# Five small reorderings in a spectral-layer-plus-FFN kernel: high parts first, scale steps on GpSimd, two preparation tables and one load moved

## The chip, the cores and the metric

The kernel runs on one core of one Trainium2 chip. The metric is the device time of one execution in microseconds (us), the median of several runs. The core's engines are named as in the profile: PE (TensorE, the matmuls), PEld (its weight loads), DVE (VectorE), ACT (ScalarE), POOL (GpSimd) and SP (SyncE, which here issues the DMA transfers). Each engine takes its instructions strictly in order; an instruction that waits holds up everything behind it on its engine.

## The reference

An input x of 8192 tokens by 448 features passes a spectral layer and a gated feed-forward layer (FFN), each with a layernorm whose scale, shift and gate come from a small condition vector c.

```python
mod = (_silu(c) @ w_mod).reshape(c.shape[0], 6, 1, -1)
sa, ca, ga, sb, cb, gb = (mod[:, n] for n in range(6))
h = _layernorm(x) * (1 + ca) + sa
x = x + ga * _A_ref(h, A_w1, A_b1, A_w2, A_b2)
h = _layernorm(x) * (1 + cb) + sb
x = x + gb * _B_ref(h, B_w_gate, B_w_up, B_w_down)

# _A_ref: rfft2 over the tokens (1 x 8192), then in 4 blocks of 112 features a complex
# two-layer MLP with biases: relu after the first layer, soft threshold (lam = 0.01)
# after the second; irfft2
# _B_ref: (gelu(x @ w_gate) * (x @ w_up)) @ w_down      448 -> 1792 -> 448
```

## The kernel before, in words

**Precision.** Matmuls run on 16-bit operands. A value that needs more is split into a high part (a cast, often on ACT) and a low part (the value minus the high part, on DVE or POOL), and both are multiplied. In the names, `hh` and `hl` are the high and low parts of the hidden layer h of the spectral MLP, `yh` and `yl` of its output y, `th` and `tl` of the transform's input t, `vh`, `gh` and `gl` of the inverse transform's input.

**The spectral stage** (about 78 to 341 us) works on 32 units (h, bt), h a half of the feature blocks and bt a group of frequencies. It is software pipelined: one step issues the transform of unit i (`stage_s2`), the first MLP layer of unit i−1 (`stage_m1`, L476 on), the second of unit i−2 (`stage_m2`), and the last transform product of unit i−3 (`stage_i1`, whose result `us` ACT copies at L589). In `stage_m1` the inner function `out` takes one bank of PSUM: ACT writes the high part with a Relu (L485), then DVE the low part (L486). The two units with bt = 0 have one frequency more (the constant term's partner) in a small bank `pmx`, and for the constant term itself ACT (L524) and DVE (L525, L526) add the biases in the same bank as the main part.

Between the steps the kernel drips in small one-off work, an entry of a list `tiny` at a time: norms of the FFN's weights, and from them scales that are powers of two. `VL` and `GL` are proxies that append an operation to that list for DVE or POOL; all these operations carry line L614. `pow2(s, bnd, p)` (L740) makes from a bound a power of two by integer arithmetic on the bits: a mask of the exponent, then a multiply-and-add. `inv_pow2` inverts such a scale with one multiply-and-add. `all_sum` (L828) adds over partitions with a small matmul that rides on another bank, whose result DVE copies out (L835). The scales are `sk` (hidden bound), `sw` (gate and up weights), `sa_act` and `isa` (activations, seven columns), `dsw`, `hs` and `ds_d` (undoing them), `dsc` (down weights).

**The FFN stage** works on 32 chunks i of two groups of tokens. Chunks 0 to 7 are in the standard form: 14 steps k of `gate_up` (L1240), two PSUM banks per step for gate and up. ACT forms gel (L1276), DVE multiplies it with the up half into x (L1281), which frees the bank; then ACT and DVE quantize x into `ac` (L1300, L1301). `down` of the chunk before (L1313 to L1315) runs after k = 2, as seven Strassen products with hooks m0, m1, m2 between them. From chunk 8 (index U0, about 745 us) on, a Strassen–Winograd form runs (`period`, L1496), with seven combined weights kept in HBM and loaded part by part (`load_part`, L1399) into a few buffers `wk`.

What else has to be done in chunks 0 to 7 stands in tables keyed by chunk and k. `start` and `steady` (into `prep`) say when each of the seven combined weights is made: `load_forms`, `form_sums` (POOL and DVE sums of raw weights `wr`), `forms_hi` (ACT) and `forms_lo` (DVE, L1728 to L1738) into `ws`, and `store_forms` to HBM (L1744). `first` says when in chunk 0 the down weights are made: `load_d8` (DMA into `dr`), `down_hi` (ACT, L1055), `down_lo` (DVE, L1059). `load_v` and `load_g` (L1028, L1020, L1022) fetch for a later chunk the inverse transform's input v, its factors g and the residual xx.

**What sets the order.** Nothing is reordered after the program is written: each engine runs its instructions in the order of the code, and SP issues the DMAs in that order too. Waits come from the framework, which tracks each buffer; for a PSUM bank that means the bank as a whole, so a reader on ACT that comes behind one on DVE in the code waits for it.

## Time and profile before

| | us |
|---|---|
| median of 3 runs (lowest, highest) | 1850.62 (1848.66, 1852.45) |
| the profiled execution | 1853.3 |
| its span (first to last instruction) | 1851.4 |
| spectral stage, from to | 78 to 341 |
| Winograd stage begins | 745 |

The profile's page gives the busy time of each engine. Its other views, which the prediction quotes, are read so. A row of the **timeline** has the start, the duration, the engine, the line, the operation, what it writes and reads, and in brackets the idle time of the engine just before it with what ended that time ("<-DVE x L1281": the engine waited for DVE's write of x on line 1281); "x8" means eight like instructions in a row, from the first one's start to the last one's end. The view of **waits** sums these idle times: in total, how often, the longest. A row of the **windows** has the busy time and the count of each engine in a stretch of time, then the granted clock of PE as a share of full speed, the busy share of the DMA engines and GB/s. Durations of pipelined instructions can overlap the next one's start a little. The page's summary by 40 slices, each 46 us, shows a steady PE from about 100 us on:

```profile
PE   7999999899999999999999999999999999999998
DVE  7788999887766667677777777777777777777755
POOL 3466878256777778777777777777777777777644
```

### The profile page before, as it was taken

What the parts mean: (1) busy time and instruction counts of PE and PEld (TensorE: products, weight loads), DVE (VectorE), ACT (ScalarE), POOL (GpSimd) and SP (SyncE); (2) the same over time, 40 slices, a digit from 0 to 9 for tenths busy, and PEclk for the clock granted to TensorE, in tenths of its full rate; (3) what the DMA queues carried; (4) which work ended last, traced back from release to release, by engine and by line L of the source; (5) the groups of instructions that cost most, each with busy time, mean ns of one, the idle gap of its engine ahead of it and who ended that gap; (6) DMA issues with size and microseconds to landing.
All of it is one profiled execution on the core that took longest, in us unless ns stands there. A gap on an engine that the chain in (4) does not pass through costs nothing.

```text
span 1851.4 us, 55998 instructions
## 1 busy us (share of the span) xinstructions
PE 1807.8 (98%) x23040; PEld 1710.9 (92%) x23040; DVE 1404.3 (76%) x2944; ACT 991.2 (54%) x1924; POOL 1316.2 (71%) x1732
## 2 busy tenths in 40 slices
PE   7999999899999999999999999999999999999998
PEld 3698989778898999999999999999999999999998
DVE  7788999887766667677777777777777777777755
ACT  5776778643434444455555555555555555555543
POOL 3466878256777778777777777777777777777644
PEclk9999999999999999999999999999999999999999
DMA  9988868654444445966666666666666666666661
GB/s 352 325 275 262 251 191 227 197 143 105 105 105 105 105 95 118 293 180 182 179 174 173 173 173 173 173 173 173 180 182 179 174 180 180 182 179 179 158 167 57
DMA packets 386232, 332.02 MB, mean 179 GB/s; under 512 B 116404, under 2 KB 364344, under 8 KB 385976
## 3 DMA queue, kind: packets, MB, share of 16 engines
q1 hardware_dynamic: 385976, 328.45, 64.4%
q8 instruction: 180, 2.95, 0.7%
q14 instruction: 76, 0.62, 0.1%
HBM read 243.32 MB, written 60.10 MB: 164 GB/s over the span
## 4 chain that ended last, share of the span: by engine, by line
PE 85%; DVE 6%; DMA 2%; POOL 2%; ACT 2%; SPq 1%; issue 1%; ACTq 0%; DVEq 0%; POOLq 0%
PE set L1496 37%; PE pgu L1240 11%; PE pdn L1313 6%; PE pdn L1315 6%; PE pdn L1314 6%; PE ps L213 2%; PE set L1313 2%; PE set L1314 2%; PE set L1315 2%; DVE y L556 1%; DVE hl L486 1%; DVE st L174 1%; PE set L1620 1%; PE pm L539 1%; PE pm L511 1%
## 5 line engine op out<-in xcount | busy, mean ns | idle before, releaser
L1496 PE MATMUL set<-nt,wk 128*128 128x128 f16 x12768 | 721.2, 219 | 3.2 <-ACT sb L1524 2.5
L1496 PEld LDWEIGHTS <-wk 128*128 128x128 f16 x12768 | 717.6, 98 | 4.8 <-issue 3.6
L1315 PE MATMUL pdn<-wd,ac 128*128 128x224 f16 x1218 | 315.5, 259 | 0.6 <-DVE ac L1301 0.6
L1313 PE MATMUL pdn<-wd,ac 128*128 128x224 f16 x1218 | 315.7, 259 | 0.0
L1314 PE MATMUL pdn<-wd,ac 128*128 128x224 f16 x1218 | 315.5, 259 | 0.0
L1240 PE MATMUL pgu<-nt,wk 128*128 128x256 f16 (+1 forms) x2464 | 269.0, 274 | 5.1 <-DVE x L1281 5.1
L1240 PEld LDWEIGHTS <-wk 128*128 128x128 f16 (+1 forms) x2464 | 226.0, 98 | 46.8 <-issue 20.9
L1545 ACT ACTIVATE gl<-c,dg 128x384 f32<-128x384 f32 x168 | 103.1, 614 | 241.4 <-DVE c L1539 238.4
L1571 DVE SCALAR_TENSOR_TENSOR ac<-x,sa_act,ac 128x896 f16<-128x896 f32 x168 | 205.0, 1220 | 35.8 <-ACT ac L1561 35.7
L1289 POOL TENSOR_TENSOR x<-x 128x128 f32<-128x128 f32 x223 | 129.5, 581 | 108.3 <-DVE x L1281 59.4
L1561 ACT ACTIVATE ac<-x,sa_act 128x896 f16<-128x896 f32 x168 | 174.8, 1040 | 54.4 <-POOL x L1292 48.2
L1290 POOL TENSOR_TENSOR x<-x 128x128 f32<-128x128 f32 x223 | 185.3, 831 | 17.5
L1359 POOL TENSOR_TENSOR cq<-cq 128x224 f32<-128x224 f32 x32 | 21.1, 658 | 246.9 <-DVE cq L1358 246.9
L1291 POOL TENSOR_TENSOR x<-x 128x128 f32<-128x128 f32 x223 | 173.1, 776 | 0.0
L1313 PEld LDWEIGHTS <-ac 128*128 128x128 f16 x1568 | 153.4, 98 | 4.9 <-issue 4.8
L1549 DVE TENSOR_TENSOR x<-c,gl 128x384 f32<-128x384 f32 x168 | 142.3, 847 | 18.4 <-ACT gl L1545 17.5
L1315 PEld LDWEIGHTS <-ac 128*128 128x128 f16 x1568 | 153.4, 98 | 0.8 <-DVE ac L1301 0.8
L1314 PEld LDWEIGHTS <-ac 128*128 128x128 f16 x1568 | 153.5, 98 | 0.1
L1292 POOL TENSOR_TENSOR x<-x 128x128 f32<-128x128 f32 x223 | 139.5, 626 | 0.0
L1533 DVE TENSOR_TENSOR c<-set,sb 128x512 f32<-128x512 f32 x168 | 115.0, 685 | 26.8 <-PE set L1496 25.3
L117 POOL TENSOR_TENSOR yl<-y,yh 128x448 fp32r<-128x448 f32 x63 | 88.2, 1417 | 54.6 <-ACT yh L115 54.3
L1276 ACT ACTIVATE gel<-pgu,dg 128x256 f32<-128x256 f32 x112 | 49.5, 471 | 140.5 <-PE pgu L1240 132.9
(346 smaller groups left out, 3786.4 us busy)
## 6 DMA issues: line engine op xcount, KB each, us to landing
wk<-wk SPq DMA_DIRECT2D x76, 1024.0 KB, 9.2
wk<-wk SPq DMA_DIRECT2D x76, 768.0 KB, 5.0
tr<-td SPq DMA_DIRECT2D x32, 448.0 KB, 4.8
vd<-us SPq DMA_DIRECT2D x64, 224.0 KB, 3.1
xx<-in_A_x SPq DMA_DIRECT2D x32, 448.0 KB, 4.2
v<-vd SPq DMA_DIRECT2D x63, 224.0 KB, 5.7
out<-x SPq DMA_DIRECT2D x31, 448.0 KB, 6.8
xt<-in_A_x SPq DMA_DIRECT2D x15, 896.0 KB, 14.9
```

What stands on the lines that cost most here:

```text
L1240: T.matmul(pgu[i, t, q][:, pr * H : (pr + 1) * H], ws[rows, n, w, tw], nts[i][rows, tn, :], start=start, stop=stop, skip_group_check=True,)
L1289: e.tensor_tensor(s1, a21, a22, ALU.add)
L1290: e.tensor_tensor(s2, s1, a11, ALU.subtract)
L1291: e.tensor_tensor(s3, a11, a21, ALU.subtract)
L1292: e.tensor_tensor(s4, a12, s2, ALU.subtract)
L1313: T.matmul(ps, ac[:, 0, ka], w[:, 0, kb], start=n == 0, stop=False)
L1314: T.matmul(ps, ac[:, 0, ka], w[:, 1, kb], start=False, stop=False)
L1315: T.matmul(ps, ac[:, 1, ka], w[:, 0, kb], start=False, stop=n == NP - 1)
L1496: T.matmul(ps2[:, pr, reg * 128 : reg * 128 + 128], slot[:, pr, hl, wt, :], nt[:, xt, :], start=start and j == 0, stop=j == len(terms) - 1 ...
L1549: V.tensor_tensor(xs[u][:, 1::3, :], cts.pop(u)[:, 1], gls.pop(u), ALU.mult)
L1561: S.activation(ac[:, 0], xs[u][:, 0:7], AF.Copy, scale=sa_act[:, t : t + 1])
L1571: V.scalar_tensor_tensor(ac[:, 1], xs.pop(u)[:, 0:7], sa_act[:, t : t + 1], ac[:, 0], op0=ALU.mult, op1=ALU.subtract)
```

## The change

It has five parts, none of which alters what is computed.

1. In `stage_m1`, `out` writes the high part and returns the low part as a function. In the units with bt = 0 both high parts of `pmx` are issued ahead of the two low parts, and ACT's bias rows (L524) ahead of the low part of their bank. The order on each engine stays the same; only who waits for whom between ACT and DVE changes.
2. `pow2` is one multiply-and-add on POOL, `inv_pow2` as well. The mask of the exponent is done on DVE: on the bound in `row_scales`, in place of the copy in `all_sum`, and on `sa_act`. Eight small operations are added on POOL.
3. The table `start`: the forms of the first combined weight are made earlier in chunk 1, most of them within the down products (m0 to m2).
4. The table `first`: the low parts 3 to 6 of the down weights, the loads 5 and 6 and the high parts 4 to 6 come later in chunk 0.
5. `load_v` and `load_g` for chunk i+3 are issued ahead of the entries of `prep` of the same k, and for i = 7 at k = 7 instead of k = 9.

```diff
                 S.activation(hhi[:BS, :, q], pv, AF.Relu)
-                V.scalar_tensor_tensor(hlo[:, :, q], pv, 0.0, hhi[:BS, :, q], op0=ALU.max, op1=ALU.subtract)
+                return lambda: V.scalar_tensor_tensor(
+                    hlo[:, :, q], pv, 0.0, hhi[:BS, :, q], op0=ALU.max, op1=ALU.subtract
+                )
...
-                for kk in range(2):
-                    out(kk, es[kk], q)
+                for low in [out(kk, es[kk], q) for kk in range(2)]:
+                    low()
...
-                out(kk, ps[:BS, : 2 * w], q)
-                if bt == 0:
+                low = out(kk, ps[:BS, : 2 * w], q)
+                if bt != 0:
+                    low()
+                else:
                     h0 = bp.tile([BS, 2], F32, tag="h0", name="h0", bufs=2)
                     for ro in range(2):
                         j = ro * NBLK + k
                         S.activation(hhi[:BS, ro, 0:1], o[ro][:, 0:1], AF.Relu, bias=hb[:, j : j + 1])
+                    low()
...
         def pow2(s, bnd, p=15):
 
             bi, si = bnd.bitcast(I32), s.bitcast(I32)
-            VL.tensor_single_scalar(si, bi, 0x7F800000, ALU.bitwise_and)
-            VL.tensor_scalar(si, si, -1.0, float((253 + p) << 23), op0=ALU.mult, op1=ALU.add)
+            GL.tensor_scalar(si, bi, -1.0, float((253 + p) << 23), op0=ALU.mult, op1=ALU.add)
 
         def inv_pow2(d, s):
-            VL.tensor_scalar(d.bitcast(I32), s.bitcast(I32), -1.0, float(254 << 23), op0=ALU.mult, op1=ALU.add)
+            GL.tensor_scalar(d.bitcast(I32), s.bitcast(I32), -1.0, float(254 << 23), op0=ALU.mult, op1=ALU.add)
...
+            bi = bnd.bitcast(I32)
+            VL.tensor_single_scalar(bi, bi, 0x7F800000, ALU.bitwise_and)
             pow2(sk, bnd, 13)
...
-                return lambda: V.tensor_copy(dst, ps[:, D : D + n])
+                return lambda: V.tensor_single_scalar(
+                    dst.bitcast(I32), ps[:, D : D + n].bitcast(I32), 0x7F800000, ALU.bitwise_and
+                )
...
+            si = sa_act.bitcast(I32)
+            VL.tensor_single_scalar(si, si, 0x7F800000, ALU.bitwise_and)
             pow2(sa_act, sa_act, 13)
...
-            ("m2", form_sums, 1),
-            ("m2", forms_hi, 1, 3),
-            (3, forms_lo, 1, 3),
...
+            ("m1", form_sums, 1),
+            ("m1", forms_hi, 1, 3, 4),
+            ("m2", forms_lo, 1, 3, 4),
...
-            4: [(pack_hi, 1), (pack_lo, 1), (down_lo, 3), (load_d8, 5)],
-            5: [(down_hi, 4)],
-            6: [(down_lo, 4), (load_d8, 6)],
-            7: [(down_hi, 5)],
-            8: [(down_lo, 5)],
-            9: [(down_hi, 6)],
-            10: [(down_lo, 6)],
+            4: [(pack_hi, 1), (pack_lo, 1)],
+            5: [(down_lo, 3), (load_d8, 5), (down_hi, 4)],
+            7: [(down_lo, 4), (load_d8, 6), (down_hi, 5)],
+            9: [(down_lo, 5)],
+            10: [(down_hi, 6)],
+            11: [(down_lo, 6)],
...
+                if k == (7 if i == NSTD - 1 else 9) and i > 0:
+                    load_v(i + 3)
+                    load_g(i + 3)
                 for fn, *args in prep.pop((i, k), []):
                     fn(*args)
...
-                if k == 9 and i > 0:
-                    load_v(i + 3)
-                    load_g(i + 3)
```

Three places show how the instructions move (line numbers of the changed kernel are some ten higher). First DVE in the spectral stage, from the sum of the weight norms (`mxa`) on to the low parts `hl` that follow the last scale, before:

```order
L835 COPY mxa<-pi_3568 128x2
L464 SCALAR_TENSOR_TENSOR zl<-ps_3588,zh_809 112x2x256
L614 TENSOR_SCALAR sw<-mxa 128x2
L464 SCALAR_TENSOR_TENSOR zl<-ps_3597,zh_810 112x2x256
L614 TENSOR_SCALAR sw<-sw 128x2
...
L464 SCALAR_TENSOR_TENSOR zl<-ps_3746,zh_812 112x2x256
L614 TENSOR_SCALAR sa_act<-sa_act 128x7 x2
L556 SCALAR_TENSOR_TENSOR y<-pm_3775,lam,t 64x224 x4
L614 TENSOR_SCALAR isa<-sa_act 128x7
L556 SCALAR_TENSOR_TENSOR y<-pm_3797,lam,t 64x224 x4
L614 TENSOR_TENSOR dsc<-dn 128x7
L486 SCALAR_TENSOR_TENSOR hl<-pm_3822,hh_813 112x2x256
```

And POOL at the same place, with the change:

```order
L117 TENSOR_TENSOR yl<-y,yh 128x448 x2
L619 TENSOR_SCALAR sw<-mxa 128x2
L619 COPY sww<-sw 64x1
L115 CAST th<-tr 128x896
L117 TENSOR_TENSOR tl<-tr,th 128x896
L619 COPY sww<-sw 64x1
L619 TENSOR_SCALAR dsw<-sw 128x2
L619 TENSOR_SCALAR hs<-sk 128x1
L619 TENSOR_SCALAR dsw<-dsw,hs 128x2
L619 COPY dg<-dsw 128x1
...
L619 TENSOR_SCALAR sa_act<-sa_act 128x7
L115 CAST th<-tr 128x896
```

The two steps of sw, those of dsw and hs, isa and one of the two of sa_act left DVE; on POOL sw, dsw, hs and sa_act now stand among the operations for th, tl and yl.

Second, DVE in chunk 1, from the first result of a down product (`cq`, seven rows for seven products) through the forms of the first combined weight (`ws`), before:

```order
L1341 TENSOR_TENSOR cq_3433<-pdn,cq_3432 128x224
L1728 SCALAR_TENSOR_TENSOR ws<-wr,sww,ws 128x3x128
L1349 TENSOR_TENSOR cq_3432<-pdn,cq_3432 128x224
...
L1368 TENSOR_TENSOR cq_3433<-pdn,cq_3432 128x224
L1281 TENSOR_TENSOR x_6750<-pgu,gel 128x2x128 x2
...
L1728 SCALAR_TENSOR_TENSOR ws<-wr,sww,ws 128x128
L1731 COPY ws<-ws 128x2x128
L1728 SCALAR_TENSOR_TENSOR ws<-wr,sww,ws 128x3x128
L1281 TENSOR_TENSOR x_6798<-pgu,gel 128x2x128
L1728 SCALAR_TENSOR_TENSOR ws<-wr,sww,ws 128x3x128
L1733 COPY ws<-ws 128x384
L1734 COPY ws<-ws 128x128
L1281 TENSOR_TENSOR x_6798<-pgu,gel 128x2x128
```

And with the change:

```order
L1351 TENSOR_TENSOR cq_3433<-pdn,cq_3432 128x224
L1738 SCALAR_TENSOR_TENSOR ws<-wr,sww,ws 128x3x128 x2
...
L1738 SCALAR_TENSOR_TENSOR ws<-wr,sww,ws 128x128
L1741 COPY ws<-ws 128x2x128
L1738 SCALAR_TENSOR_TENSOR ws<-wr,sww,ws 128x3x128 x2
L1743 COPY ws<-ws 128x384
L1744 COPY ws<-ws 128x128
L1367 TENSOR_TENSOR cq_3433<-pdn,cq_3432 128x224
...
L1291 TENSOR_TENSOR x_6805<-pgu,gel 128x2x128
L1738 SCALAR_TENSOR_TENSOR ws<-wr,sww,ws 128x3x128
L1746 COPY ws<-ws 128x128
L1738 SCALAR_TENSOR_TENSOR ws<-wr,sww,ws 128x256
```

The forms that stood around the first x of the second pair of banks now stand ahead of `cq` of the down product; the next forms took their place between the x of that pair.

Third, SP at the last standard chunk (the stores `wk_73<-ws` of the last combined weight, the loads of Winograd weights, and v, g, xx), before:

```order
L1480 DMA_TRANSPOSE nt<-pk 128x5x128 x4
L1744 DMA wk_73<-ws 64x4x384 x4
L1399 DMA wk_3420<-wk_62 128x8x512
L1399 DMA wk_3420<-wk_63 128x8x384
L1028 DMA v<-vd 128x2x224 x2
L1020 DMA g<-cgm 128x256
L1022 DMA xx<-in_A_x 128x896
L1399 DMA wk_3421<-wk_64 128x8x512
```

And with the change:

```order
L1490 DMA_TRANSPOSE nt<-pk 128x5x128 x4
L1038 DMA v<-vd 128x2x224 x2
L1030 DMA g<-cgm 128x256
L1032 DMA xx<-in_A_x 128x896
L1754 DMA wk_73<-ws 64x4x384 x4
L1409 DMA wk_3420<-wk_62 128x8x512
L1409 DMA wk_3420<-wk_63 128x8x384
L1409 DMA wk_3421<-wk_64 128x8x512
```

The v, g and xx transfers went ahead of the four stores and two loads; what stands behind them is the same.

More of the change, by code (lines that the diff above doesn't have):

```diff
@@ L1748, in spectral_geglu @@
             ("m0", form_sums, 0),
-            ("m0", forms_hi, 0),
-            ("m1", forms_lo, 0),
-            ("m1", forms_hi, 2),
-            ("m2", forms_lo, 2),
-            ("m2", form_sums, 1),
-            ("m2", forms_hi, 1, 3),
-            (3, forms_lo, 1, 3),
-            (3, forms_hi, 4),
-            (4, forms_lo, 4),
-            (4, form_sums, 2),
-            (4, forms_hi, 5),
-            (5, forms_lo, 5),
-            (5, forms_hi, 6),
-            (5, store_forms, 0),
-            (6, forms_lo, 6),
-            (6, forms_hi, 7),
-            (7, forms_lo, 7),
-            (7, forms_hi, 8),
-            (8, forms_lo, 8),
-            (9, store_forms, 1),
+            ("m0", forms_hi, 0, 2),
+            ("m1", forms_lo, 0, 2),
+            ("m1", form_sums, 1),
+            ("m1", forms_hi, 1, 3, 4),
+            ("m2", forms_lo, 1, 3, 4),
+            ("m2", form_sums, 2),
+            ("m2", forms_hi, 5),
+            (3, forms_hi, 6),
+            (4, forms_lo, 5, 6),
+            (4, store_forms, 0),
+            (4, forms_hi, 7),
+            (5, forms_lo, 7),
+            (6, forms_hi, 8),
+            (7, forms_lo, 8),
+            (8, store_forms, 1),
         ]
```

## The prediction

> **What bounds the kernel now.** I read the page's busy shares first, then the view of waits of the tensor engine (PE), then its timeline and the windows around each wait, and last the rows of the engines that each wait names.
>
> ```profile
> PE 1807.8 (98%) x23040; PEld 1710.9 (92%) x23040; DVE 1404.3 (76%) x2944; ACT 991.2 (54%) x1924; POOL 1316.2 (71%) x1732
> ...
> 821.12 29.80 PE set L1496 x532
> ...
> PE pgu L1240 <- DVE x L1281: 5.1, 7, 1.2
> PE pm L539 <- DVE hl L486: 4.2, 7, 1.7
> PE pw L819 <- ACT us L589: 4.2, 2, 2.2
> PE set L1496 <- ACT sb L1524: 2.5, 1, 2.5
> ...
> 250.00:275.00 25.00, 25.00 (x266) 24.31 (x265) 24.48 (x48) 21.36 (x40) 19.92 (x15) 1.00 0.77 212
> ```
>
> The first row is the page's; the second is a piece of the chain of work that ended last; the next four are PE's waits (total, times, longest); the last is a window of 25 us, in the order PE, weight load, DVE, ACT, POOL. PE is busy 1807.8 of 1851.4 us, so all its idle time is 43.6 us. The Strassen stage runs 532 matmuls in 29.80 us, 56 ns each, with nothing between them, and in the middle of the spectral stage PE is busy 25.00 of 25 us. So a microsecond of PE idle that goes early is carried to the end, and no more than 43.6 can go. The four rows of waits are 16.0 us together, and the change aims at them; the other 27.6 us lie at places that it does not touch.
>
> A second cost sits behind some of these waits: the granted clock (the last but two column).
>
> ```profile
> 158.70:162.10 3.40, 3.40 (x26) 2.81 (x26) 3.26 (x9) 0.63 (x1) 3.24 (x4) 0.50 0.91 230
> 244.00:247.40 3.40, 3.17 (x18) 2.61 (x18) 3.35 (x8) 1.97 (x5) 3.33 (x3) 0.50 0.58 142
> 752.60:756.00 3.40, 3.40 (x35) 3.40 (x34) 2.31 (x2) 3.40 (x10) 3.40 (x5) 0.50 1.10 334
> 170.00:173.40 3.40, 3.37 (x45) 3.08 (x45) 2.39 (x6) 2.04 (x4) 3.32 (x4) 1.00 0.54 135
> ```
>
> After the waits that end at 157.18, 243.73 and 752.47 PE runs one window of 3.4 us at 0.50; after the wait of 1.99 us that ends at 170.03 it does not. Half speed over 3.4 us is 1.7 us of work lost where PE is the bound. I take it that a drop goes with the wait ahead of it.
>
> **Part 1: constant-term units.** Two units have the extra column (bt = 0); their `stage_m1` now issues a high part (ACT) before the low part (DVE) that reads the same bank.
>
> ```profile
> ACT hh L524 <- DVE hl L486: 3.0, 4, 0.8
> ACT hh L485 <- DVE hl L486: 2.8, 2, 1.7
> ...
> 148.33 3.72 DVE L556 SCALAR_TENSOR_TENSOR y<-pm,lam,t 64x224 f32<-64x224 f32 x8
> 156.59 0.97 ACT L589 COPY us<-pi 128x448 f32<-128x448 f32 x2
> 157.18 0.34 PE L819 MATMUL pw<-onesb,sq 128*128 128x1 bf16 x8 [2.19 <-ACT us L589]
> 170.03 0.34 PE L819 MATMUL pw<-onesb,sq 128*128 128x1 bf16 x8 [1.99 <-ACT us L589]
> ```
>
> The first two rows are ACT's waits between 148 and 172 us. Per unit ACT waits for DVE once at L485 (1.7 us in one, 2.8 − 1.7 = 1.1 in the other) and twice at L524 (3.0 / 4 = 0.75 each): 3.2 us in the first unit, 2.6 in the second. Behind them on ACT stand the cast of yh and the copy us, and on us waits PE. Without them PE could go on at 157.18 − 3.2 = 153.98; it is ready at 157.18 − 2.19 = 154.99. Next late is DVE's y, which ends at 148.33 + 3.72 = 152.05; yh and us behind it, at about 1 us each (0.97), end near 154, so again in time. In the second unit us allows 170.03 − 2.6 = 167.43, against 168.04. Both waits go, with 0.6 to 1.0 us to spare: 2.19 + 1.99 = **−4.2**. No instruction is added. Bounds: half of it (−2.1) if a second dependence holds ACT, and −5.9 if the half-speed window at 158.70 is gained as well; I take none of that 1.7, since PE waits again at 170.03, so what it loses at half speed before is time that it would have waited.
>
> **Part 2: steps of the scales on POOL.** Eight integer steps on tiles of up to seven columns leave DVE; the masks stay on it, and one of them rides on a copy that is there anyway.
>
> ```profile
> 227.46 1.45 DVE L614 TENSOR_SCALAR sw<-sw 128x2 int32<-128x2 int32 x1
> 236.63 1.28 DVE L614 TENSOR_SCALAR sa_act<-sa_act 128x7 int32<-128x7 int32 x2
> 239.68 1.19 DVE L614 TENSOR_SCALAR isa<-sa_act 128x7 int32<-128x7 int32 x1
> 242.78 0.17 DVE L614 TENSOR_TENSOR dsc<-dn 128x7 f32<-128x7 f32 x1
> 242.98 0.69 DVE L486 SCALAR_TENSOR_TENSOR hl<-pm,hh 112x512 f16<-112x512 f32 x1
> ...
> 227.00 1.89 POOL L117 TENSOR_TENSOR tl<-tr,th 128x896 f16<-128x896 f32 x1
> 233.90 1.78 POOL L614 TENSOR_SCALAR dsw<-dsw,hs 128x2 f32<-128x2 f32 x1 [4.50 <-DVE hs L614]
> 240.97 0.33 POOL L614 TENSOR_SCALAR sa_act<-sa_act,dsw 128x7 f32<-128x7 f32 x1
> ...
> 240.91 0.65 PE L457 MATMUL ps<-s,tl 128*112 128x128 f16 x8 [0.27 <-POOL tl L117]
> 243.73 0.27 PE L539 MATMUL pm<-w2h,hl 112*128 112x224 f16 x1 [1.40 <-DVE hl L486]
> ```
>
> A step of 0.17 us on DVE takes 1.19 to 1.45 us while POOL runs a large operation: sw, begun at 227.46, ends at 228.91, with POOL's tl (227.00 + 1.89 = 228.89). From 235 to 243 DVE has no idle time, so each step stands ahead of hl at 242.98. Isa (1.19) and half of the pair sa_act (0.64) go: hl begins at 241.15 at the latest, 1.83 us earlier, and PE asks for it 1.40 us earlier. That wait goes. POOL gets sw, dsw, hs and sa_act ahead of the tl that PE waited 0.27 us for; POOL's own idle time of 4.50 us there (it waited for DVE's hs, which it now makes itself) holds them, at 0.33 us as in the quiet row. I take −1.3 of the waits (1.40 + 0.27, less 0.4 for steps stretched on POOL) and −1.7 for the half-speed window at 244.00: **−3.0**. Bounds: −3.4 with both waits whole, and 0 if the waits only move to POOL; beyond that the slower rival, below.
>
> [...]
>
> **Parts 3 and 4: chunks 0 and 1 of the FFN.** A gate-up bank is freed by DVE's x (L1281), which queues behind low down weights (chunk 0) or forms (chunk 1).
>
> ```profile
> 391.61 4.96 PE L1240 MATMUL pgu<-nt,wk 64*128 64x256 f16 x45 [0.29 <-DVE x L1281]
> 402.74 1.03 PE L1240 MATMUL pgu<-nt,wk 64*128 64x256 f16 x9 [1.14 <-DVE x L1281]
> 398.61 1.04 ACT L1055 ACTIVATE wd<-dr,dsc 128x896 f16<-128x896 f32 x1 [1.37 <-DMA dr<-sd]
> ...
> 438.53 0.48 PE L1240 MATMUL pgu<-nt,wk 64*128 64x256 f16 x5 [1.17 <-DVE x L1281]
> 460.44 2.77 PE L1240 MATMUL pgu<-nt,wk 64*128 64x256 f16 x25 [0.92 <-DVE x L1281]
> 433.74 2.45 DVE L1728 SCALAR_TENSOR_TENSOR ws<-wr,sww,ws 128x384 f16<-128x384 f32 x1
> 436.44 1.43 DVE L1728 SCALAR_TENSOR_TENSOR ws<-wr,sww,ws 128x384 f16<-128x384 f32 x1
> 419.48 0.39 DVE L1349 TENSOR_TENSOR cq<-pdn,cq 128x224 f32<-128x224 f32 x1 [2.17 <-PE pdn L1315]
> ```
>
> Chunk 0: the small wait at 391.61 goes (−0.29). The one at 402.74 does not: `load_d8(6)` now stands behind the later low part 4 on SP and lands about where ACT already waited 1.37 us for it (398.61), and ACT's gel and DVE's x queue behind that cast. Moved by one or two positions it costs between 0 and a further 2 us. I take **−0.4**, between −1.4 (both gone) and +1.0. Chunk 1: forms of 2.45 and 1.43 us between two x are the wait of 1.17. They move into the down products, where DVE sat 2.17 us idle before one row alone. The wait at 460.44 lies behind the chunk's last forms, which now come a k or two sooner. Of 1.17 + 0.92 I take **−1.6** (0 to −2.1): the forms of k = 4 now stand between the x of one pair, so something remains.
>
> **Part 5: inverse input earlier.** At i = 7, v, g and xx now stand ahead of four stores of forms and two loads of Winograd weights on SP.
>
> ```profile
> 740.91 4.27 SPq L1028 DMA_DIRECT2D v<-vd  x2
> 751.00 0.94 ACT L1120 CAST vh<-v 128x896 fp32r<-128x896 f32 x1 [2.81 <-DMA v<-vd]
> 752.47 7.82 PE set L1496 x108
> 735.92 2.86 SPq L1744 DMA_DIRECT2D wk<-ws  x4
> 738.00:750.00 12.00, 11.99 (x148) 10.69 (x146) 11.38 (x30) 3.42 (x6) 8.36 (x13) 1.00 1.03 294
> ```
>
> ACT waits 2.81 us for v with sb, PE's releaser, queued behind; PE waits 2.49 and runs its next 108 matmuls in 7.82 us, where 108 × 56 ns is 6.05: 1.77 us more. Issued at about 735.9, v lands five us earlier, and the stall is gone: 2.49 + 1.77 = 4.26. But the DMA engines are full (share 1.03) and the same bytes stand in the queue: the store and the weights of the second Winograd unit move back by v's 4.27 us of issuing and a little for g and xx. PE sits idle for none of them now (11.99 of 12 us busy up to 750), but how much earlier they land than they are wanted no row tells. Behind v in the queue nothing changes, so the third unit's weights land as late as before while PE comes to them 4 us sooner. A new wait may thus cost anything from nothing to all of the 4.26; I take half, **−2.1**, as neither end has the nearer row.
>
> **Sum.** −4.2 − 3.0 − 0.4 − 1.6 − 2.1 = −11.3. The profiled execution took 1853.3 us (span 1851.4), 2.7 over the median of 1850.6, and would take 1842.0; from the median it is 1839.3, which I predict. A measurement of this kernel tells about 0.2%, 3.7 us, from no change.
>
> **The rivals.** *Half speed stays* (0.12): the window at 244 or 752 comes of a shorter wait too, or of something else there. For it: 170.03 shows that a wait of 1.99 us needn't bring one, so wait and drop are not one to one. Price: 1.7 + 1.77, less the half that part 5 discounts, about 2.6: 1841.9 to 1842.8. [...]
>
> *The moved transfers take the waits' place* (0.12): chunk 0 loses 1.0 for the late down weights, part 5 and chunk 1 bring nothing. For it: full DMA engines and SP's fixed order. Sum −4.2 − 3.0 + 1.0 = −6.2: 1844.4.
>
> *Given back in the drain* (0.10): what parts 1 and 2 gain is lost again when the spectral stage ends, because its last transfers and not PE set that end. For it: of the 27.6 us of idle time elsewhere some lies there. Against it: PE, busy 25.00 of 25 us, is the bound ahead of it. Left are 0.4 + 1.6 + 2.1 = 4.1: 1846.5, at the bound of 0.2%.
>
> *The waits have twins* (0.07): the change does not do what it says, since a second condition ends within 0.3 us of each removed wait; 1850 ± 2.
>
> *Slower* (0.08): POOL's eight steps each meet a DVE operation and take 1.78 us, as dsw does at 233.90. That is 14.2 us, less POOL's idle 4.50: th, tl and yl come 9.7 us late and PE, busy 25.00 of 25 us, has no slack to take it. With −8.3 of the other parts it is +1.4, and +4.8 with the two half-speed windows that waits of this size bring by the rows above: 1855.4. The sign turns where a step takes over (4.50 + 8.3 − 3.4) / 8 = 1.2 us. Against it: 0.33 us at 240.97.
>
> **How the numbers follow.** The forecast keeps 0.51; its own range is 1834 to 1843. Faster by over 0.2% are the forecast, the first rival, most of the second (0.10) and half of the third (0.05): 0.78. Within 0.2%: 0.02 + 0.05 + 0.07 = 0.14. Slower: 0.08. All bounds at their best give −5.9 − 3.4 − 1.4 − 2.1 − 4.3 = −17.1, or 1833.5. The range of 1833.5 to 1848.5 leaves out the slower rival and the twins, 0.15, and little else.
>
> **What would show it.** PE's wait on us (4.2 us) gone from the view of waits, and with it ACT's on hl; no wait of PE over 1 us at 243 and a clock of 1.00 in the window behind; POOL's small steps at 0.2 to 0.4 us, not 1.8; no PE wait near 438; at 752 no row of 2.5 us, but one of 1 to 2 us with a DMA of wk behind it. I am wrong if PE waits for th, tl or yl in the spectral stage, if ACT waits over 2 us for dr near 400, or if the half-speed windows stay with their waits gone.

## The result, and the profile after

| | us |
|---|---|
| before, median of 5 runs (lowest, highest) | 1850.51 (1848.22, 1852.45) |
| changed, median of 5 runs (lowest, highest) | 1839.09 (1836.23, 1842.32) |
| ratio, 95% interval | 0.9939 (0.9922 to 0.9955) |
| profiled execution of the changed kernel (span) | 1839.5 (1837.4) |

The changed kernel is faster by 0.6%, 11.4 us, and its median is 0.2 us from the predicted 1839.3. How far that is luck is told below.

PE's busy time on the page and its view of waits, after:

```profile
PE 1804.2 (98%) x23040; PEld 1708.0 (93%) x23040; DVE 1400.6 (76%) x2934; ACT 991.9 (54%) x1924; POOL 1320.0 (72%) x1740
...
PE pgu L1250 <- DVE x L1291: 3.2, 3, 1.6
PE pm L544 <- DVE hl L486: 2.3, 5, 1.5
PE pi L590 <- DVE hl L486: 1.1, 2, 0.9
PE set L1506 <- DMA wk<-wk: 1.8, 2, 1.0
...
PE pw L825 <- ACT us L594: 0.7, 1, 0.7
```

The four rows at which the change aimed fell from 16.0 to 6.2 us (5.1 to 3.2 for x, 4.2 to 2.3 for hl, 4.2 to 0.7 for us, 2.5 to none for sb), while a new row of 1.8 us for the weights `wk` came and a wait on hl grew from 0.3 us (at L585) to 1.1 us (L590).

Both profiles hold the same 23040 matmuls in the same order. So the start of each matmul after, less the start of the same one before, is PE's lead at that place, and the growth of the lead over a stretch is what was gained there. I did this for the two first profiles, and again for a second profile of each kernel (below, `before_again` and `after_again`). Times of places are those of the kernel before.

| place | predicted | first pair | second pair |
|---|---|---|---|
| up to 144 us, one step of part 2 | 0 | −1.2 | −1.7 |
| part 1, 144 to 172 | −4.2 | −4.2 | −5.3 |
| part 2, 228 to 256 | −3.0 | −3.9 | −2.8 |
| drain, 325 to 362, not touched | 0 | −1.6 | −2.2 |
| part 4, chunk 0, 362 to 408 | −0.4 | +0.9 | +0.5 |
| part 3, chunk 1, 408 to 465 | −1.6 | −2.1 | −2.1 |
| part 5, Winograd entry, 742 to 770 | −2.1 | −1.8 | −2.1 |
| the rest | 0 | −0.1 | −0.3 |
| sum | −11.3 | −14.0 | −16.0 |

The first row is nearly all chance. Of the change only the step of `sk` lies there, at 102 us; with part 2 a wait of PE on hl behind it is 1.5 us instead of 1.7. The thirteen other profiles of this study lie between 0.0 and −3.9 us there against the first profile of before, and the second profile of the same kernel at −1.5. Without this row the pairs give −12.8 and −14.3, and the medians −11.4 here and −13.0 in the second measurement. One row has the wrong sign (chunk 0) and one was not foreseen (the drain).

### The profile page after: what moved, and what is told of

It is laid out like the page before. It is cut to its first block, busy times and chain, and to the rows that moved or that the text cites. A ratio compares the mean times of both kernels' runs of the same rounds, so it can differ in the third digit from the quotient of the medians.

```text
span 1837.4 us, 55986 instructions
## 1 busy us (share of the span) xinstructions
PE 1804.2 (98%) x23040; PEld 1708.0 (93%) x23040; DVE 1400.6 (76%) x2934; ACT 991.9 (54%) x1924; POOL 1320.0 (72%) x1740
## 4 chain that ended last, share of the span: by engine, by line
PE 87%; DVE 6%; DMA 2%; POOL 2%; ACT 2%; issue 1%; SPq 0%; ACTq 0%; DVEq 0%; POOLq 0%
PE set L1506 37%; PE pgu L1250 11%; PE pdn L1323 6%; PE pdn L1325 6%; PE pdn L1324 6%; PE ps L213 2%; PE set L1325 2%; PE set L1323 2%; PE set L1324 2%; DVE y L561 1%; PE set L1630 1%; PE pm L513 1%; DMA wk<-wk 1%; PE ps L451 1%; PE pm L515 1%
```

## The experiments

All of them are compared by PE's lead at each place, which resolves 0.1 us where a median of a few runs resolves about 1.5.

### Part 1 taken back

```diff
-                for low in [out(kk, es[kk], q) for kk in range(2)]:
-                    low()
+                for kk in range(2):
+                    out(kk, es[kk], q)
```

and likewise for the bias rows.

> The changed kernel with part 1 taken back (high and low parts of the constant-term units in the old order). Theory: part 1 is worth 4.6 us, because in the two traces PE's lead grows from 0.7 to 5.4 us between 150 and 170 us. Then PE's two waits on us (2.2 and 2.0 us) return, a half-speed window returns behind the first, the profiled span is 4 to 5.5 us longer than the changed kernel's 1837.4, and the drain near 331 us keeps its short waits. Rival: the spectral stage is paced elsewhere and gives part 1's lead back, so that the span is within 2 us of 1837.4.

Measured: 1844.74 us, ratio 0.9974 (0.9963 to 0.9986), span 1842.7. PE's rows of this kernel at the two waits, and the windows behind them:

```profile
155.79 0.34 PE L820 MATMUL pw<-onesb,sq 128*128 128x1 bf16 x8 [2.19 <-ACT us L589]
...
168.59 0.34 PE L820 MATMUL pw<-onesb,sq 128*128 128x1 bf16 x8 [2.00 <-ACT us L589]
...
156.72:160.13 3.41, 3.41 (x26) 2.55 (x24) 2.90 (x7) 1.07 (x2) 3.33 (x4) 0.50 0.75 188
170.37:173.78 3.41, 3.41 (x24) 2.83 (x21) 3.17 (x8) 0.69 (x2) 3.25 (x4) 0.50 0.93 248
```

Both waits are back to a hundredth, and this time both have a half-speed window behind them. Between 144 us and the end of the second window PE loses 6.8 us against the changed kernel and gets none of it back before 325 us: the spectral stage carries the lead. So the part is worth more than the 4.2 us of its waits, and what it is worth depends on the half-speed windows.

### Part 2 taken back

```diff
-            GL.tensor_scalar(d.bitcast(I32), ...)
+            VL.tensor_scalar(d.bitcast(I32), ...)
```

and `pow2` and the masks as before.

> The changed kernel with part 2 taken back (all steps of the scales on DVE again, masks as before). Theory: part 2 is worth 3.8 us at 230 to 250 us; hl near 237 to 238 us comes late again (PE wait about 1.4 us) and a half-speed window may follow it; the span is 3 to 4.5 us longer. Rival for the drain: the 1.9 us that PE won between 325 and 360 us, which the prediction did not have, also belong to part 2 (its POOL or DVE order reaches further than thought): then the span is 5 to 6.5 us longer.

Measured: 1841.73 us, ratio 0.9958 (0.9942 to 0.9974). One row of PE and two of DVE, in this kernel:

```profile
237.34 0.27 PE L544 MATMUL pm<-w2h,hl 112*128 112x224 f16 x1 [1.40 <-DVE hl L486]
...
230.24 1.27 DVE L619 TENSOR_SCALAR sa_act<-sa_act 128x7 int32<-128x7 int32 x2
...
233.29 1.19 DVE L619 TENSOR_SCALAR isa<-sa_act 128x7 int32<-128x7 int32 x1
```

The steps of 1.2 us and the wait of 1.40 are back. No half-speed window followed, and PE loses 2.8 us at this place. In `before_again` (below), which has the same wait of 1.39 us, none followed either, so the half-speed window is no fixed part of what part 2 is worth. The waits in the drain stay short (0.45 and 0.47 us at L538), so the drain's gain isn't part 2's alone, and the rival there falls.

### Part 3 taken back

> The changed kernel with part 4 taken back (the old table for chunk 0's down weights). Theory: part 4 costs time, since in the changed kernel ACT waits 1.9, 1.3 and 1.3 us for the moved loads into dr, PE waits 1.63 us at 391 us and runs a window at half speed behind it: without part 4 that wait and window go, waits of 0.3, 0.2 and about 1.1 us come back, and the span is 1 to 2.5 us shorter. Rival (the prediction): part 4 gains 0.4 us, so the span is about 0.4 us longer.

The kernel that ran is another than its expectation says: it has the old table `start` (part 3 taken back), the new table `first`, and leaves out the mask on `sa_act`, so that this scale is no power of two. It says nothing on part 4 and is read here for part 3. Measured: 1839.33 us, ratio 0.9950 (0.9935 to 0.9965). PE's waits in chunk 1:

```profile
426.75 0.48 PE L1248 MATMUL pgu<-nt,wk 64*128 64x256 f16 x5 [1.16 <-DVE x L1289]
...
448.57 1.68 PE L1248 MATMUL pgu<-nt,wk 64*128 64x256 f16 x15 [0.92 <-DVE x L1289]
```

The waits of 1.17 and 0.92 us of the kernel before are back as 1.16 and 0.92, where the changed kernel has one of 0.69. PE loses 2.0 us in chunk 1, the 2.1 that both pairs show. This profile also loses 2.5 us at the Winograd entry, which bears on part 5.

### Part 5 taken back

> The changed kernel with part 5 taken back (v, g and xx behind the stores and the weights again). Theory: PE's wait on sb of about 2.5 us returns near 741 us with a half-speed window in most phases, PE's waits of 0.99 and 0.85 us on the Winograd weights go, and the span is 1.5 to 2.7 us longer. Rival: the waits on the weights stem from the DMA volume and stay; then the span is 3 to 4.5 us longer.

Measured: 1840.76 us, ratio 0.9955 (0.9939 to 0.9971); the profiled execution was the fastest of the four, 1838.5. Its waits at the Winograd entry:

```profile
PE set L1506 <- ACT sb L1534: 1.1, 1, 1.1
PE set L1506 <- DMA wk<-wk: 1.1, 1, 1.1
```

The wait on sb is 1.1 us and not 2.5, with no half-speed window behind it, and a wait on the weights stays: at the entry this profile loses 0.1 us against the changed kernel. Neither theory gave that. Of three profiles with the old order, the wait on sb was 2.5, 2.6 (`before_again`) and 1.1 us; in the third, SP's transposes took 0.6 to 0.8 us less and v landed at least 0.5 us sooner after its issue. With the new order the entry is as uneven: PE's first wait on the weights is 0.9 to 1.3 us in four of the eight profiles that have part 5 as it is, and 1.7 to 2.1 us in the other four. In `undo4` it is 2.13 us with a half-speed window behind it, and the entry ends 0.7 us later than in the first profile of before. Against that profile, the entry brings between 1.8 us and −0.7 us with part 5, and between 1.7 and −0.3 us without it. By the medians of this kernel and of the changed one (1837.4 to 1839.1) part 5 is worth 1.7 to 3.4 us, but the intervals overlap, and this profile loses 1.8 us behind 770 us, at eleven waits of 0.11 to 0.12 us each in the Winograd stage that no other shows and whose cause is open. What part 5 is worth is therefore not settled.

### Part 4 taken back

```diff
-            4: [(pack_hi, 1), (pack_lo, 1)],
-            5: [(down_lo, 3), (load_d8, 5), (down_hi, 4)],
-            7: [(down_lo, 4), (load_d8, 6), (down_hi, 5)],
+            4: [(pack_hi, 1), (pack_lo, 1), (down_lo, 3), (load_d8, 5)],
+            5: [(down_hi, 4)],
+            6: [(down_lo, 4), (load_d8, 6)],
...
```

> The changed kernel with the table of chunk 0 alone taken back (low down weights early again; the forms of chunk 1 stay moved). In the changed kernel ACT waits 1.9, 1.3 and 1.3 us for loads into dr between 380 and 390 us and PE 1.63 us at 391. Theory A: these waits come of part 4, since its loads stand behind later low parts; then the span is 1 to 2.5 us shorter than the changed kernel's 1837.4 and PE has no wait over 1.2 us between 380 and 400. Theory B (the prediction): the table gains 0.4 us; PE then waits about 1.1 us once at a later step, and 0.2 to 0.3 us twice, and the span is within 1 us.

Measured: 1835.91 us, ratio 0.9927 (0.9912 to 0.9941). In the changed kernel, ACT's high parts of the down weights (L1065) and PE's row behind them, and the window that follows:

```profile
382.69 1.04 ACT L1065 ACTIVATE wd<-dr,dsc 128x896 f16<-128x896 f32 x1 [1.88 <-DMA dr<-sd]
...
387.08 0.85 ACT L1065 ACTIVATE wd<-dr,dsc 128x672 f16<-128x672 f32 x1 [1.33 <-DMA dr<-in_B_w_down]
389.23 1.04 ACT L1065 ACTIVATE wd<-dr,dsc 128x896 f16<-128x896 f32 x1 [1.30 <-DMA dr<-sd]
...
391.15 4.16 PE L1250 MATMUL pgu<-nt,wk 64*128 64x256 f16 x25 [1.63 <-DVE x L1291]
...
392.34:395.75 3.41, 3.41 (x16) 2.35 (x14) 3.37 (x5) 0.36 (x1) 3.01 (x3) 0.50 0.01 2
```

And PE in the same chunk with the old table:

```profile
372.68 4.85 PE L1250 MATMUL pgu<-nt,wk 128*128 128x256 f16 x43 [1.07 <-DVE x L1291]
...
388.35 2.77 PE L1250 MATMUL pgu<-nt,wk 64*128 64x256 f16 x25 [0.56 <-DVE x L1291]
```

Theory A holds: part 4 takes time. Chunk 0 takes 1.6 us less with the old table than in the changed kernel's first profile and 0.3 less than in its second. The two differ by the half-speed window alone: it follows the wait of 1.63 in the first profile and not the 1.67 in the second. Against the first profile of before, chunk 0 takes 0.7 to 1.3 us more in the five profiles that have the new table and a half-speed window there, and between 0.4 less and 0.2 more in the three without the window; with the old table (four profiles) it is never slower, and up to 0.9 us faster.

### The cause in chunk 0: high part 6 one step later

```diff
-            10: [(down_hi, 6)],
-            11: [(down_lo, 6)],
+            11: [(down_hi, 6)],
+            12: [(down_lo, 6)],
```

`best1` has this edit, with one at the Winograd entry that is read in the next part.

> As the last, but with the new table for chunk 0, in which the high part 6 comes one step later (with low part 6 behind it). Theory: in the changed kernel ACT waits 1.33 and 1.30 us in high part 6 for the late load into dr, with a gel behind it on which DVE's x and so PE's 1.63 us at 391 hang; one step later the load has landed before ACT comes to it, and the wait of PE falls below 0.5 us, with no half-speed window behind it. Rival: PE's wait hangs on DVE's low part ahead of x and stays over 1 us. The entry into the Winograd stage as in the last kernel.

The DVE row that frees PE in the changed kernel, and ACT and PE of `best1` in chunk 0:

```profile
390.67 0.42 DVE L1291 TENSOR_TENSOR x<-pgu,gel 128x256 f32<-128x256 f32 x1 [1.47 <-ACT gel L1286]
...
390.82 1.77 ACT L1065 ACTIVATE wd<-dr,dsc 128x672 f16<-128x672 f32 x2
...
385.25 7.75 PE L1250 MATMUL pgu<-nt,wk 128*128 128x256 f16 x68 [0.76 <-DVE x L1291]
```

ACT no longer waits before high part 6, and PE's 1.63 us are gone; one wait of 0.76 earlier in the chunk is left. Chunk 0 takes 2.4 and 1.1 us less than in the changed kernel's two profiles. So PE's wait in the changed kernel came through ACT: a high part that waits for its transfer, with gel queued behind it, and DVE's x behind gel.

### The Winograd entry: stores last

`best1` and `best2` (the old table for chunk 0) also change the order of SP's transfers: v, the second unit's weights, g and xx, the third unit's weights, and the four stores last. Of the edit the lines for the stores are shown; the load of g and xx moves by a like one.

```diff
-                at_k = (n, NFT + k) if type(k) is int and k < 0 else (1 + n, k)
+                late = n == NP - 1 and fn is store_forms and args == [1]
+                at_k = (n, NFT + k) if type(k) is int and k < 0 else (1 + n, 12 if late else k)
```

> Parts 1, 2 and 3 of the change and the load of v from part 5, with the old table for chunk 0, and at the entry into the Winograd stage the load of v first, then the two loads for the second Winograd unit, then g and xx (xx held SP up 1.8 us in the changed kernel), the two loads for the third unit, and the four stores last. Theory: PE's waits for these weights (1.2 and 0.8 us with the old table) come of the transfers ahead of them in SP's order, so both go or fall below 0.3 us, v still lands in time, and the time is 1 to 2 us below the kernel with the old table alone (0.9927 of the kernel before), some 4 to 5 us below the changed kernel. Rival: the DMA engines are full there, so only the order of landing changes and one of the waits stays.

Measured: `best2` 1843.26 us, ratio 0.9963 (0.9951 to 0.9974); `best1` 1841.63, 0.9954 (0.9936 to 0.9971). Both are slower than the changed kernel. ACT and PE of `best1`:

```profile
740.73 0.59 ACT L1534 COPY sb<-set 128x512 f32<-128x512 f32 x1 [9.09 <-DMA wk<-ws]
...
741.37 1.91 PE L1506 MATMUL set<-nt,wk 128*128 128x128 f16 x14 [6.60 <-ACT sb L1534]
```

Both theories are wrong. The waits on the weights are gone, but ACT's first copy into sb waits 9.09 us for the stores out of ws, and PE 6.60 us behind it. In the code ws lies in a pool that is closed before the pool of sb is opened; by this wait sb lies in memory of ws, and the stores must have read it first. So the stores can't come last: ACT and PE wait for them. No view of the kernel before shows this, since there they were done in time.

### Both corrections

`best3` has the later high part 6 and, on SP, v, the four stores, the second unit's weights, and then g and xx.

> The changed kernel with high part 6 of the down weights one step later (as in best1), and at the entry into the Winograd stage v, the four stores, the two loads for the second unit, and only then g and xx. Theory: PE's 1.63 us at 391 fall below 0.8 us and the half-speed window behind them goes; without the 1.8 us that SP waited for xx, PE's wait of about 0.9 us on the second unit's weights goes, and since the stores stay ahead of sb there is no stall like the 6.6 us of best1 and best2. The time is 2 to 4 us below the changed kernel: 0.991 to 0.993 of the kernel before. Rival: the DMA engines are full, so what the second unit's weights win the third unit's lose, and only chunk 0 gains: 0.9925 to 0.994.

Measured: 1833.61 us (1832.01 to 1835.31), ratio 0.9906 (0.9892 to 0.9921), a median below that of both kernels, though the interval still touches that of the changed kernel's second measurement (from 0.9914, below). PE of `best3`:

```profile
384.33 7.75 PE L1250 MATMUL pgu<-nt,wk 128*128 128x256 f16 x68 [0.59 <-DVE x L1291]
...
737.73 1.96 PE L1506 MATMUL set<-nt,wk 128*128 128x128 f16 x32 [1.21 <-DMA wk<-wk]
```

Chunk 0 takes 2.8 and 1.5 us less than in the changed kernel's two profiles. At the entry the rival holds: the wait on the weights is still 1.21 us with the 1.8 us of SP's wait taken out, and the entry gains 0.2 us.

### Two profiles of the same kernels

> The kernel before, profiled once more, to see what differs between two profiles of one kernel. Theory: PE's waits on us (2.2 and 2.0 us), hl near 243 (1.4), x in chunks 0 and 1 and sb at 752 (2.5) return within 0.2 us each; the start (up to 100 us) and the half-speed windows behind waits of 1.6 to 2.5 us differ, since the grid of windows lies anew in each run. The wait of 1.74 us near 342, which no run with part of the change showed, returns if the change as a whole removed it, and does not if it was chance.

> The changed kernel once more, on the chip of the two kernels above, as their measure: 0.994 of the kernel before (0.9922 to 0.9955 in the first measurement), PE's waits as in its first profile within 0.3 us, except at the start and for the half-speed windows.

Measured: 1850.89 us for the one run of `before_again`; `after_again` 1837.40 us, ratio 0.9934 (0.9914 to 0.9955). The waits of `before_again`:

```profile
PE pgu L1240 <- DVE x L1281: 4.3, 7, 1.2
PE pw L819 <- ACT us L589: 4.2, 2, 2.2
...
PE set L1496 <- ACT sb L1524: 2.6, 1, 2.6
PE pm L533 <- DVE y L556: 2.0, 2, 1.5
```

They return within 0.2 us, but for one wait on x in chunk 0 (1.14, now 0.33). The drain's wait (1.74, now 1.52) returns too. It is 0.45 us in eleven profiles with all or part of the change, but 1.75 in `best1`, which has parts 1 and 2. So the drain's gain is tied to the change in most executions and to no part of it by any run here; why is open. In `after_again` PE's waits behind 100 us return within 0.3 us, except the 0.90 us at L590, which is not there.

### The slower rival: longer steps on POOL

```diff
+                for _ in range(5):
+                    G.tensor_scalar(pad[:, : d.shape[1]], s, -1.0, c, op0=ALU.mult, op1=ALU.add)
                 G.tensor_scalar(d, s, -1.0, c, op0=ALU.mult, op1=ALU.add)
```

> The changed kernel with five more like operations into a scratch tile ahead of each of the eight steps on POOL, so that a step takes about 1.2 us instead of 0.2: about 8 us more on POOL in the spectral stage; nothing else computed differs. This prices the rival that ends slower. Prediction's rival: POOL's lateness beyond its idle time reaches PE by th, tl and yl, so PE loses some 8 - 4.5 = 3.5 us or more in waits of ps on th or tl and of pi on yl, and the part is no longer worth anything. Theory of slack: POOL has idle time ahead of each yl (1.8, 0.5, 0.6, 1.2, 0.9 us in the changed kernel), which takes all but the steps that stand two or three together (dsw and hs; isa); PE loses under 2 us.

Measured: 1844.17 us, ratio 0.9970 (0.9959 to 0.9980), span 1841.5. The padding of a step on POOL, what DVE runs beside it, and PE's largest waits:

```profile
226.86 2.76 POOL L750 TENSOR_SCALAR pad<-sk 128x1 int32<-128x1 int32 x5
228.02 1.27 DVE L944 SCALAR_TENSOR_TENSOR wk<-raw,sw,wk 128x1024 f16<-128x1024 f32 x1
...
235.25 0.26 PE L451 MATMUL ps<-s,th 128*112 128x128 f16 x1 [1.73 <-POOL th L115]
237.23 0.65 PE L457 MATMUL ps<-s,tl 128*112 128x128 f16 x8 [0.87 <-POOL tl L117]
```

Of the seven paddings between 220 and 260 us four take 1.3 to 1.4 us, and 2.2 to 2.8 us the three where DVE runs its operation on raw and wk, and PE loses 4.4 us between 228 and 325 us, 3.9 of it in waits on th and tl: more than part 2 gains. The slack theory (under 2 us) falls, and the rival's mechanism is right: POOL's lateness beyond its idle time reaches PE. Its size is not. With the stretched paddings the eight steps take 15.8 us and not the 9.6 us meant, so this run carries the load that the prediction's rival assumed, 14.2 us. PE loses 4.4 us by it and not 9.7, and the kernel stays faster than before. So steps of that duration would have cost part 2 its gain, and not have made the change a loss.

### Which waits bring half speed

```diff
+            for _ in range(8 + 2 * (u // NP - 9) // 3 if u > U0 + 6 and u % NP == 2 else 0):
+                seed(u - 1)
             on(u - 1, seed)
```

> The changed kernel with a copy within PSUM that PE waits for (seed) repeated 8 to 22 times, once in each Winograd chunk from 9 on, all to the same values: each stalls PE once, by lengths from near nothing to some 4 us. It measures which idle times bring a half-speed window. Theory from the traces: PE's idle time within one window of a fixed grid of 3.41 us decides, and over about 1.65 us (half of it) the next window runs at 0.50; under 1.5 us none does. A stall of 1.7 to 3.3 us then brings one in some phases of the grid and not in others, one over 3.4 us always. [...]

Measured: 1954.5 us; 23 stalls of 1.05 to 6.59 us. Three of them on PE, and the windows of 3.41 us on the grid that the half-speed windows keep:

```profile
1025.17 1.10 PE L1506 MATMUL set<-nt,wk 128*128 128x128 f16 x9 [2.22 <-ACT set L1538]
...
1221.32 0.89 PE L1506 MATMUL set<-nt,wk 128*128 128x128 f16 x13 [3.38 <-ACT set L1538]
...
1270.05 1.25 PE L1506 MATMUL set<-nt,wk 128*128 128x128 f16 x18 [3.38 <-ACT set L1538]
...
1021.81:1025.23 3.42, 1.20 (x20) 1.02 (x18) 1.32 (x2) 3.17 (x10) 2.38 (x4) 1.00 0.95 292
1025.23:1028.64 3.41, 3.41 (x33) 3.41 (x33) 2.13 (x3) 2.10 (x4) 2.24 (x4) 0.50 1.16 301
...
1216.37:1219.78 3.41, 1.57 (x27) 1.39 (x25) 1.74 (x3) 3.13 (x10) 2.81 (x5) 1.00 0.77 226
1219.78:1223.19 3.41, 1.87 (x33) 1.87 (x33) 0.85 (x2) 3.32 (x8) 0.64 (x2) 1.00 1.17 305
1223.19:1226.60 3.41, 3.41 (x31) 3.13 (x30) 2.38 (x3) 0.29 (x1) 3.11 (x5) 1.00 0.72 196
1267.57:1270.99 3.42, 0.94 (x17) 0.94 (x17) 0.43 (x1) 3.23 (x10) 0.41 (x1) 1.00 1.15 303
1270.99:1274.40 3.41, 3.41 (x23) 3.24 (x21) 1.73 (x3) 1.21 (x3) 2.59 (x4) 0.50 0.62 159
```

The two stalls of 3.38 us are equal in length. The grid cuts the first into 1.84 and 1.54 us of idle time, and no half speed follows; the second has 2.48 us in one window, and the next runs at 0.50, as behind the stall of 2.22 us that lies in one window. From 100 us to the tail at 1830 in `before` and `after`, and in the windows of `stalls` above and the one from 1073.01, seven windows at full speed hold 1.89 to 3.18 us of idle time, and the next one ran at 0.50 each time (those from 104.07, 155.27, 356.66 and 749.19 in `before`, 344.55 in `after`, 1021.81 and 1267.57 in `stalls`). Of the seven with 1.54 to 1.84 us, three were followed by 0.50 (1.63 and 1.71 us in `after`, 1.66 in `before`) and four by 1.00 (1.74 in `before`; 1.54, 1.74 and 1.84 in `stalls`); in `before` and `after` none was with 1.17 us or less. Idle time is not all of it, though: earlier, the windows from 76.76 in `before` and from 74.90 in `after` ran at 0.50 behind windows in which PE is busy 3.40 and 3.41 us. The theory is right that the idle time within one window counts in these stalls, and not their length; its threshold of 1.65 us does not hold, since half speed followed 1.63 us and not 1.84.

Behind a window that itself ran at 0.50, less idle time went with another: 1.11 us in `best3`, 1.17 in `before` (from 360.07) and 1.62 in `after` (from 347.96) were followed by 0.50 again, 0.53 in `after` (from 351.38) and 0.23 in `before` (from 244.02) by 1.00. Two windows of `best3` in the drain, the first with the 1.11 us:

```profile
348.63:352.04 3.41, 2.30 (x17) 1.88 (x18) 2.77 (x7) 2.57 (x6) 0.00 (x0) 0.50 0.07 7
352.04:355.45 3.41, 3.41 (x18) 2.43 (x16) 3.41 (x5) 1.70 (x2) 0.00 (x0) 0.50 0.81 252
```

## Why the prediction was right

**The bound and the carrying** held: every gain at a place is still there at the end, and the rows without a part of the change gain 0.4 us or less, but for the start and the drain.

**Part 1, −4.2: the sum right, its terms not.** Removing the waits gave less than 2.19 + 1.99: in the first unit 0.67 us on us is left, and the wait on hl ahead of it (L590) grew from 0.30 to 0.90 us, because ACT came late to hh and to the copies:

```profile
150.65 1.06 ACT L814 ACTIVATE sq<-xt 128x1024 bf16<-128x1024 f32 x1 [2.44 <-DMA xt<-in_B_w_up]
...
155.10 0.34 PE L825 MATMUL pw<-onesb,sq 128*128 128x1 bf16 x8 [0.67 <-ACT us L594]
```

ACT waits 2.44 us for a transfer, a step that the prediction did not look for. And the half-speed window at 158.70, which it priced at nothing because PE waits again at 170, was worth something: PE's lead grows by 1.6 us across it, gives back 0.4 by 166, and does not shrink at 170. The two errors cancel, which is luck. The wait for the transfer differs from one execution to the next: in the three profiles with part 1 where it is 0.3 us or less (`undo2`, `undo5`, `stalls`) this stretch gains 6.1 us against the first profile of before, about the prediction's bound of 5.9, and 3.5 to 5.6 us in the eight where it is 1.1 us or more.

**Part 2, −3.0 against −3.9 and −2.8: the mechanism right, two terms mis-sized.** The waits on hl and tl went with the steps. The rows of the new steps on POOL:

```profile
220.78 0.19 POOL L619 TENSOR_SCALAR sw<-mxa 128x2 int32<-128x2 int32 x1
...
232.75 0.21 POOL L619 TENSOR_SCALAR isa<-sa_act 128x7 int32<-128x7 int32 x1
```

They take 0.2 us, not the 0.33 of the row that it went by (that one multiplies by a second tile, the steps by constants), so nothing of the waits was lost to POOL and the deduction of 0.4 us falls away. Taken by the lead, the waits were worth 2.8 us and not 1.3: 0.5 at tl, 1.8 at hl, and 0.8 at two small waits on DVE near 234 (0.17 and 0.29 us in the timeline) that the prediction did not count, less 0.2 that a wait near 253 takes back. The half-speed window, priced at 1.7 us, was worth 1.1 in the first pair and nothing in the second, where neither kernel has one. Here too the sum came near by errors that cancel. On these tiles the 0.19 to 0.22 us on POOL are near DVE's 0.14 and 0.17 for such a step while POOL waited (233.58 and 232.77, before).

**Part 3, −1.6 against −2.1.** Right in its mechanism; of 1.17 + 0.92 + 0.36 us, 0.69 is left, and it is the wait that was foreseen, on the forms between the x of one pair. The third wait of 0.36 was not counted, and is worth 0.6 by the lead.

**Part 4, −0.4 against +0.9 and +0.5: wrong.** The failed step is its choice of a value. The chain was named (the load behind the later low part, ACT's high part waiting for it, gel and x behind that) and bounded at +1.0, but taken as a small gain. The later load made ACT wait 1.88, 1.33 and 1.30 us, PE 1.63 us, and in some executions a half-speed window follows. `best1` and `best3` show that the high part on ACT is the link. By `undo4_first` the part costs 0.3 us, and 1.6 with the window.

**Part 5, −2.1 against −1.8 and −2.1.** The stall of 2.5 us and the half-speed window went, and the two waits on weights that were to come are there:

```profile
736.50 4.58 PE L1506 MATMUL set<-nt,wk 128*128 128x128 f16 x74 [0.99 <-DMA wk<-wk]
741.93 1.24 PE L1506 MATMUL set<-nt,wk 128*128 128x128 f16 x19 [0.85 <-DMA wk<-wk]
```

The value was a halfway choice and hit by chance: without part 5 the same place was once as fast (`undo5`), and with it once slower than before (`undo4`).

**What was missing.** The drain's 1.6 to 2.2 us. The sum of the places is 1 to 3 us more than the medians moved; the start and the half-speed windows differ by as much from one execution to the next, but that they are the reason is not shown. That the median came within 0.2 us of the forecast is luck; what the runs bear out is which waits go in parts 1 to 3 and by what.

**The rivals.** "Half speed stays" fell: the window behind 243 us is at 1.00 in every profile with part 2. It is at 1.00 in `before_again` and `undo2` as well, though, so half speed was not a sure cost of the wait. "The moved transfers take the waits' place" came true for chunk 0, near its price of 1.0, and in part for part 5. "Slower" has the right mechanism but not the size: the steps take 0.2 us, and with steps as long as it assumed PE lost 4.4 us and not 9.7.

## What to carry to other kernels

In this kernel, which PE bounds at 98%, a wait of PE that went was in three places worth its length and 0.2 to 0.4 us more by the lead (1.8 us for the 1.40 on hl, 0.5 for the 0.27 on tl, 0.6 for the 0.36 in chunk 1), and in two places there were 1.1 and 1.3 us on top where a half-speed window had followed. So the waits with such a window behind them, of 2.19, 1.40 and 2.49 us in the first profile, are where to look first. Ask of each moved instruction what is queued behind it on its own engine: here a high part whose casts wait 1.33 and 1.30 us for transfers cost PE 1.63 us, more than the work that was moved out of its way gained, and one step later they no longer waited. Compare two profiles of one program by the starts of the same matmuls: the lead at each place shows what a part is worth at a tenth of a microsecond where medians can't, and a second profile of the same kernel shows which of it is chance.

## What the runs showed of the hardware

Within a profile the half-speed windows began whole steps of 3.413 us apart: in `before` (107.48, 158.68, 244.02, 360.07 and 752.60 us) 15, 25, 34 and 115 of them, in `after` (105.62, 347.96, 392.34) 71 and 13, in `stalls` (1025.23, 1270.99) 72. Against the work this grid lay elsewhere from one execution to the next: behind the end of PE's first wait on us the window began 1.50 us later in `before` (157.18 to 158.68) and 0.93 in `undo1` (155.79 to 156.72). Of two stalls of 3.38 us in `stalls`, the one with 2.48 us in one window was followed by half speed, and the one cut into 1.84 and 1.54 was not. The same wait cost more in the execution where a half-speed window followed it: 1.1 us more behind hl at 243 us, 1.3 us more in chunk 0.

A small integer step took 0.19 to 0.22 us on POOL in the changed kernel. In `pool_padded` five like ones took 2.21 to 2.78 us in the three paddings that lie beside DVE's operation on raw and wk (2.76 beside the one at 228.02), and 1.29 to 1.36 in the four that lie beside none. In the kernel before DVE's steps took 1.45 and 1.19 us beside POOL's tl (227.00 and 238.96), and 0.17 and 0.14 us (232.77, 233.58) while POOL waited. So in these rows the steps of either engine took longer beside these operations of the other, and a duration from a quiet row is the shortest that they show; why is open.
